# Sign of the first two w_in blocks: a second integer instruction on VectorE, or a sign tile by ScalarE and a product by GpSimd

## The chip, the cores and the metric

The kernel runs on one core of one Trainium2 chip. The time is device microseconds from the first to the last instruction, with what lies around them, and one number is the median of several runs. The profile's names are used for the engines: PE (TensorE), DVE (VectorE), ACT (ScalarE), POOL (GpSimd) and SP (SyncE, which here only issues DMAs).

## The reference

Three layers follow each other:

```python
a = softmax(phi, axis=seq)                      # (4, 8, 576, 32)
k_m, v_m = a^T @ k, a^T @ v                     # 32 memory rows of each head
attn = softmax(q @ k_m^T / 8) @ v_m             # (4, 8, 576, 64)
x = attn.transpose(0, 2, 1, 3).reshape(2304, 512)
h = x @ w_in;  g = h * sigmoid(h);  x = g @ w_out          # 512 -> 2048 -> 512
# then a top-2 mixture of 8 experts, 512 -> 1024 -> 512, on x
```

The weights `w_in` (512 x 2048) and `w_out` (2048 x 512) arrive as 64-bit floating point numbers. The kernel reads them as pairs of 32-bit words and makes 32-bit floating point numbers of them on the chip. That conversion is what the change touches.

## The kernel before, in words

The sequence is worked through batch by batch (`b` = 0 to 3). For a batch, the memory rows are formed (`phi_top`, `phi_max`, `memory`, `memory_t`; `KVT[b]` holds them transposed), the attention weights are computed in two column ranges of 256 and 320 tokens (`scores`, `softmax_a`, `softmax_b`, `turn`, `halves`), and w_in is multiplied by the memory's values once per batch (`project`), so that the first MLP product (`mlp_h`, 32 steps of a batch) takes attention weights straight into the 2048 hidden columns. `mlp_x` multiplies the activated hidden rows by w_out. PE keeps precision by splitting its operands into a high and a low part (`ah`, `wph`/`wpl`, `gh`/`gl`, `woh`/`wol`), each product being three matmuls.

w_in is cut into `NP` = 8 blocks of 256 columns, `WI[i]`, and each block into two pieces of 128 x 512 numbers. w_out is cut into 16 pieces of 128 x 512. `stage` (L204) loads a piece as 512 word pairs per partition into one of four `st` buffers. A piece is then narrowed: `shrink` (L209) runs two ScalarE instructions, one on the low words (`lw`), one on the high words (which go into the result `m` as a scaled magnitude); `join` (L215) is a VectorE integer instruction that shifts `m` left by 3 and ors the low bits in. The sign is still missing. It comes in one of two ways, chosen by `own` in `narrow` (L223):

- `own=True` (all of w_in): `sign` (L219), a second VectorE integer instruction, takes the sign bit out of the staged high words and ors it into `m`.
- `own=False` (all of w_out): ScalarE writes the sign of the staged number in bf16 into the tile `cg` (one buffer, L227), and GpSimd multiplies `m` by `cg` (L232).

Block 0 of w_in is not narrowed through `narrow_win` but written out by hand at L858 to L870, between the pieces of the first batch's attention, since the first `project(0, 1)` needs it. `narrow_win(1)` follows at L885, the remaining blocks are narrowed from a table of steps while the MLP of batch 0 runs. After narrowing, a block is written to `win_d` by a DMA that GpSimd issues (L868, L250), for the later batches.

The order on each engine is made from the program's order by a scheduler when the kernel is built; `tc.issue_after` places an instruction behind another one. Each engine works through its own list in order.

Of the kernel before, what the change touches and what calls it, by code (L numbers as in the profile page):

```python
# [6 lines left out]
F32 = mybir.dt.float32  # L7
F32R = mybir.dt.float32r
BF16 = mybir.dt.bfloat16
I32 = mybir.dt.int32  # L10
U32 = mybir.dt.uint32
AF = mybir.ActivationFunctionType
# [32 lines left out]
def body(ctx, tc, a):  # L45
    nc = tc.nc
    pe, act, dve, pool, sp = nc.tensor, nc.scalar, nc.vector, nc.gpsimd, nc.sync
# [8 lines left out]
    def psum(tag, bufs):  # L56
        return ps.tile([128, 512], F32, name=tag, tag=tag, bufs=bufs)
# [19 lines left out]
    ap_ = att.enter_context(tc.tile_pool(name="att", bufs=1, side="right"))  # L77

    AT = {}
    QT, KV, KX, PH, KVT, AH, AU = {}, {}, {}, {}, {}, {}, {}  # L80
# [65 lines left out]
    def memory_t(b):  # L146
        pt = psum("aux", 2)
        for t in range(2):
            pe.transpose(pt[:, t * 128:(t + 1) * 128], src[:, t].rearrange("p g d -> p (g d)"), ident)
        KVT[b] = m1.tile([128, 2, 128], F32, name="kvt", bufs=2)  # L150
        act.activation(KVT[b].rearrange("p t j -> p (t j)"), pt[:, :256], AF.Copy)

    def heads(p, b, t, moving):
        for h in range(4):
# [4 lines left out]
    def scores(b, i):  # L159
        t0, w = T0[i], TW[i]  # L160
        p = [psum("aux", 2)[:, :w] for g in range(2)]
        heads(p, b, 0, lambda h: QT[b, h][:, t0:t0 + w])
        if i == 0:
            AT[b] = ap_.tile([128, 2, S // M, M], F32, name="sct", tag="big", bufs=1)
        for g in range(2):
            dve.transpose(AT[b][:, g].rearrange("p a m -> p (a m)")[:, t0:t0 + w], p[g])

    def softmax_a(b, t0, w):
        n = w // M
        t = AT[b][:, :, t0 // M:t0 // M + n, :]  # L170
        mx = ap_.tile([128, 2, S // M], F32, name="smx")[:, :, :n]
        dve.tensor_reduce(mx, t, axis=AX.X, op=OP.max)
        last = dve.tensor_sub(t, t, mx[:, :, :, None].to_broadcast([128, 2, n, M]))
        act.activation(t, t, AF.Exp, scale=0.125)
        return last
# [33 lines left out]
    def shrink(t, m):  # L209
        low = ap_.tile([128, 512], I32, name="lw", bufs=1)  # L210
        act.activation(low, t[:, :, 0].bitcast(U32), AF.Copy, scale=LOW, bias=LOWB)  # L211
        act.activation(m, t[:, :, 1].bitcast(F32), AF.Copy, scale=2.0 ** -112)
        return low

    def join(m, low):  # L215
        mi = m.bitcast(I32)
        return dve.scalar_tensor_tensor(mi, mi, 3, low, op0=OP.logical_shift_left, op1=OP.bitwise_or)  # L217

    def sign(t, m):  # L219
        mi = m.bitcast(I32)  # L220
        dve.scalar_tensor_tensor(mi, t[:, :, 1], -2 ** 31, mi, op0=OP.bitwise_and, op1=OP.bitwise_or)

    def narrow(t, m, own=False):  # L223
        low = shrink(t, m)
        if not own:
            g = ap_.tile([128, 512], BF16, name="cg", bufs=1)
            act.activation(g, t[:, :, 1].bitcast(F32), AF.Sign)  # L227
        join(m, low)
        if own:
            sign(t, m)  # L230
        else:
            pool.tensor_mul(m, m, g)  # L232


    WP, WI, ST = {}, {}, {}
# [10 lines left out]
    def narrow_win(i):  # L246
        WI[i] = m1.tile([128, 4, PW], F32, name="wi", tag="wi", bufs=2)
        for g, t in enumerate(ST.pop(("i", i))):
            narrow(t, WI[i][:, 2 * g:2 * g + 2, :].rearrange("p r f -> p (r f)"), True)
        pool.dma_start(win_d[i], WI[i].rearrange("p r f -> p (r f)"))  # L250

    def project(i, n):
# [19 lines left out]
    def narrow_wout(i):  # L272
        w = ap_.tile([128, DM], F32, name="wo", bufs=2)
        narrow(ST.pop(("o", i)), w)
        act.activation(woh[i], w, AF.Copy)
        (pool if i % 2 else dve).tensor_sub(wol[i], w, woh[i].bitcast(F32))
# [581 lines left out]
    first = ST.pop(("i", 0))  # L858
    WI[0] = m1.tile([128, 4, PW], F32, name="wi", tag="wi", bufs=2)
    parts = [WI[0][:, 2 * g:2 * g + 2, :].rearrange("p r f -> p (r f)") for g in range(2)]  # L860
    narrow(first[0], parts[0], True)
    memory_t(0)
    scores(0, 0)
    low = shrink(first[1], parts[1])
    with tc.issue_after(softmax_a(0, T0[0], TW[0]).ins):
        joined = join(parts[1], low)
    sign(first[1], parts[1])
    pool.dma_start(win_d[0], WI[0].rearrange("p r f -> p (r f)"))  # L868
    with tc.issue_after(joined.ins):
        softmax_b(0, T0[0], TW[0])  # L870
# [13 lines left out]
    with tc.issue_after(ready.ins):  # L884
        narrow_win(1)  # L885
# [6 lines left out]
    for i in range(1, NP):  # L892
        if i + 1 < NP:
            at(max(0, 4 * i - 7), fetch_win, i + 1)
            at(max(0, 4 * i - 4), narrow_win, i + 1)
        at(4 * i - 2, project, i, 1)
# [5 lines left out]
    for b in range(1, B):  # L902
# [6 lines left out]
        if b == 1:  # L909
            for step, fn, g in ((7, phi_top, 0), (9, phi_max, 0), (9, phi_top, 1), (11, phi_max, 1),  # L910
                                (12, memory, 0), (13, memory, 1)):
                at(step, fn, b, g)
            for step, fn, *more in ((16, memory_t), (20, scores, 0), (23, scores, 1), (24, softmax_a, 0, S),
                                    (25, softmax_b, 0, S), (27, split, 0, 0, S), (28, split, 1, 0, S)):
                at(step, fn, b, *more)
        else:
            at(s + 8, phi_top, b, 0)
            at(s + 9, phi_top, b, 1)
            at(s + 10, phi_max, b, 0)
            at(s + 10, phi_max, b, 1)  # L920
            at(s + 11, memory, b, 0)
            at(s + 11, memory, b, 1)
            at(s + 12, memory_t, b)
            at(s + 15, scores, b, 0)
            at(s + 16, scores, b, 1)
            at(s + 17, softmax_a, b, 0, S)
            at(s + 20, softmax_b, b, 0, S)
            at(s + 22, split, b, 0, 0, S)
            at(s + 24, split, b, 1, 0, S)
# [4 lines left out]
    for b in range(B - 1):  # L934
# [7 lines left out]
        if b == 1:  # L942
            j = TILES.index((b, 4))
# [37 lines left out]
    while s < total + LAG + 6:  # L981
# [4 lines left out]
        if s in (2 * SB, 4 * SB):  # L986
            b = s // SB - 1
# [83 lines left out]
```

## Time and profile before

| | |
|---|---|
| median of 3 runs | 845.61 us (845.02 to 845.68) |
| the profiled execution, its own time | 845.91 us |
| its span, first to last instruction | 844.1 us, 14185 instructions |
| PE busy | 807.1 us, 96% |
| DVE busy | 496.8 us, 59% |
| ACT busy | 360.8 us, 43% |
| POOL busy | 209.9 us, 25% |
| PE's granted clock, mean | 0.983 |

The shares of the table are over the whole span. The profile also has the span in 40 slices, each about 21 us long. PE is busy for 4, 5 and 8 tenths of the first three and for nearly all of every one behind them; its clock is at half in the second. DVE and ACT are busiest in slices 2 to 7, in which the 32 pieces of w_in and w_out are narrowed. The change lies in the first 42 us.

### The profile page before, as it was taken

To read this page: it belongs to the slowest core of one execution; us is meant where nothing else is said; L and a number is where in the kernel's file an instruction comes from. 1 tells how busy PE (TensorE), PEld (TensorE's weight loads), DVE (VectorE), ACT (ScalarE), POOL (GpSimd) and SP (SyncE) were. 2 spreads that over 40 slices of the span, in tenths; PEclk is the share of its full clock that TensorE was granted. 3 is DMA by queue.
4 is the path that set the end of the run, shared out by engine and by line. 5 is a ranking of instruction groups with operands and counts; after the bars stand their busy time and mean duration, and the time that the engine had idled before them with its cause. 6 is when DMAs were issued, how large, how long until landed. Compare 5 with 4: busy or idle time off the path is not lost.

```text
span 844.1 us, 14185 instructions
## 1 busy us (share of the span) xinstructions
PE 807.1 (96%) x5260; PEld 691.4 (82%) x5260; DVE 496.8 (59%) x1178; ACT 360.8 (43%) x856; POOL 209.9 (25%) x237
## 2 busy tenths in 40 slices
PE   4589999999999999999999999999999999999996
PEld 2267678878887888887988989989989899898995
DVE  4898996884268747655724555354553654546521
ACT  3689975444333454553414433324332333233410
POOL 1254530021000400400541504215133142241301
PEclk9599999999999999999999999999999999999999
DMA  9889852543074215232456893765748647586201
GB/s 304 291 295 325 283 217 71 159 131 94 7 229 153 51 51 151 57 82 50 113 138 187 257 257 124 185 237 171 188 169 221 241 139 160 198 220 196 74 4 53
DMA packets 85935, 137.84 MB, mean 163 GB/s; under 512 B 14045, under 2 KB 48349, under 8 KB 85856
## 3 DMA queue, kind: packets, MB, share of 16 engines
q1 hardware_dynamic: 74656, 104.41, 40.9%
q0 software_dynamic: 11200, 32.43, 12.7%
q8 instruction: 43, 0.70, 0.4%
q14 instruction: 36, 0.29, 0.1%
HBM read 106.13 MB, written 31.26 MB: 163 GB/s over the span
## 4 chain that ended last, share of the span: by engine, by line
PE 81%; DVE 9%; ACT 4%; DMA 3%; issue 2%; POOL 1%; SPq 0%; POOLq 0%; ACTq 0%; DVEq 0%
PE x L706 25%; PE x L313 18%; PE x L682 13%; PE h L682 12%; PE h L288 9%; PE aux L157 2%; DMA st<-moe_w_out 1%; DVE th L293 1%; DVE gl L298 1%; DMA kx<-kx 1%; ACT lw L211 1%; POOL wo L232 1%; DMA st<-moe_w_in 1%; DVE mx L113 1%; DVE wo L217 1%
## 5 line engine op out<-in xcount | busy, mean ns | idle before, releaser
L706 PE MATMUL x<-w,gh 128*128 128x512 f32 (+1 forms) x608 | 188.1, 390 | 0.0
L706 PEld LDWEIGHTS x<-w,gh 128*128 128x128 f32 (+1 forms) x608 | 112.4, 186 | 24.3
L682 PE MATMUL h<-xh,w 128*128 128x304 f32 (+4 forms) x512 | 118.7, 304 | 0.0
L706 PE MATMUL x<-w,gl 128*128 128x512 f32 (+1 forms) x304 | 118.5, 390 | 0.0
L682 PE MATMUL x<-xh,w 128*128 128x304 f32 (+4 forms) x512 | 118.1, 302 | 0.0
L288 PE MATMUL h<-ah,wph 128*128 128x320 f32 (+1 forms) x512 | 109.3, 302 | 3.8 <-DVE th L293 1.7
L313 PE MATMUL x<-gh,woh 128*128 128x512 f32 x256 | 105.5, 412 | 0.0
L288 PEld LDWEIGHTS h<-ah,wph 128*128 128x128 f32 x512 | 90.0, 192 | 18.2 <-ACT ah L195 3.6
L721 POOL DMA_INDIRECT out<-y,tab x40 | 41.9, 1049 | 243.1 <-DVE y L716 187.3
L313 PE MATMUL x<-gl,woh 128*128 128x512 f32 x256 | 100.7, 393 | 0.7 <-DVE gl L298 0.7
L313 PE MATMUL x<-gh,wol 128*128 128x512 f32 x256 | 101.2, 395 | 0.0
L293 DVE SCALAR_TENSOR_TENSOR th<-th,h 128x256 f32<-128x256 f32 (+1 forms) x128 | 57.6, 450 | 53.0 <-ACT th L291 52.5
L497 POOL DMA_INDIRECT tab_d<-rows,slot x36 | 40.6, 1128 | 191.3 <-DVE slot L494 177.9
L682 PEld LDWEIGHTS h<-xh,w 128*128 128x128 f32 x512 | 87.3, 188 | 0.6
L682 PEld LDWEIGHTS x<-xh,w 128*128 128x128 f32 x512 | 87.4, 188 | 0.0
L291 ACT ACTIVATE th<-h 128x256 f32<-128x256 f32 (+1 forms) x128 | 52.3, 408 | 73.4 <-PE h L288 71.3
L288 PE MATMUL h<-ah,wpl 128*128 128x256 f32 (+1 forms) x256 | 76.6, 300 | 2.3 <-DVE wpl L264 2.3
L682 PE MATMUL x<-xl,w 128*128 128x304 f32 (+4 forms) x256 | 78.0, 305 | 0.0
L682 PE MATMUL h<-xl,w 128*128 128x304 f32 (+4 forms) x256 | 77.7, 303 | 0.0
L297 ACT ACTIVATE gh<-th 128x256 fp32r<-128x256 f32 x128 | 53.3, 416 | 55.7 <-DVE th L293 55.3
L298 DVE TENSOR_TENSOR gl<-th,gh 128x256 fp32r<-128x256 f32 x120 | 55.1, 459 | 32.0 <-ACT gh L297 28.1
L716 DVE SCALAR_TENSOR_TENSOR y<-x,tab,ex 128x512 f32<-128x512 f32 (+2 forms) x35 | 26.2, 749 | 71.4 <-PE x L706 71.4
(189 smaller groups left out, 1342.0 us busy)
## 6 DMA issues: line engine op xcount, KB each, us to landing
w2s<-moe_w SPq DMA_DIRECT2D x32, 512.0 KB, 8.5
wi<-win_d SPq DMA_DIRECT2D x24, 512.0 KB, 5.1
w1s<-moe_w SPq DMA_DIRECT2D x24, 512.0 KB, 6.2
kv<-kv SPq DMA_DIRECT2D x16, 520.0 KB, 7.3
st<-moe_w_in SPq DMA_DIRECT2D x16, 512.0 KB, 5.2
st<-moe_w_out SPq DMA_DIRECT2D x16, 512.0 KB, 5.9
xs_d<-ex SPq DMA_DIRECT2D x25, 256.0 KB, 3.6
x_d<-xs SPq DMA_DIRECT2D x36, 128.0 KB, 2.4
```

The lines of the kernel that those rows point to most:

```text
L157: pe.matmul(p[g][h * M:(h + 1) * M], KVT[b][r, t, h * M:(h + 1) * M], moving(h)[r], start=True, stop=True)
L288: pe.matmul(p[:, :w], wt[:, g, c:c + 128], AH[b, g][at][:, t0:t0 + w], start=(n == 0), stop=(n == 5))
L291: act.activation(th[:, :w], p[:, :w], AF.Tanh, scale=0.5)
L293: dve.scalar_tensor_tensor(u[:, :w], th[:, :w], 1.0, p[:, :w], op0=OP.add, op1=OP.mult)
L297: act.activation(gh, u[:, :256], AF.Copy)
L298: last = (pool if b == 0 and (2 * f + i) % 4 == 0 else dve).tensor_sub(gl, u[:, :256], gh.bitcast(F32))
L313: pe.matmul(X2[key], held, moved, start=(f == 0 and n == 0), stop=(f == NF - 1 and n == 2))
L497: st = pool.indirect_dma_start(out=tab_d, out_offset=bass.IndirectOffsetOnAxis(ap=slot[:, j, k:k + 1], axis=0), in_=rows.bitcast(I32)[:, j ...
L682: pe.matmul(p[:, :w], wt[:, d, c], x[:, d, r], start=(n == 0), stop=(n == 11))
L706: mm = pe.matmul(p, g, w[:, f, :], start=(n == 0), stop=(n == (15 if both else 23)))
L716: done = dve.scalar_tensor_tensor(y, p[:P], w, EX[k, j], op0=OP.mult, op1=OP.add)
L721: st = pool.indirect_dma_start(out=a["out"], out_offset=bass.IndirectOffsetOnAxis(ap=TAB[k][:P, j, 0:1], axis=0), in_=y, in_offset=None, b ...
```

## The change

Blocks 0 and 1 of w_in (four pieces) get their sign in the way of w_out: ScalarE's sign in bf16 into the one `cg` buffer and GpSimd's product. The blocks 2 to 7 stay with VectorE's integer instruction. In the hand-written part, the sign of the first piece is placed behind `memory_t`'s copy on ScalarE. Lines above L223 keep their numbers; those behind are 4 higher (8 behind the hand-written part).

```diff
+    def signs(t):
+        g = ap_.tile([128, 512], BF16, name="cg", bufs=1)
+        act.activation(g, t[:, :, 1].bitcast(F32), AF.Sign)
+        return g
+
     def narrow(t, m, own=False):
         low = shrink(t, m)
-        if not own:
-            g = ap_.tile([128, 512], BF16, name="cg", bufs=1)
-            act.activation(g, t[:, :, 1].bitcast(F32), AF.Sign)
-        join(m, low)
         if own:
+            join(m, low)
             sign(t, m)
         else:
+            g = signs(t)
+            join(m, low)
             pool.tensor_mul(m, m, g)
...
-            narrow(t, WI[i][:, 2 * g:2 * g + 2, :].rearrange("p r f -> p (r f)"), True)
+            narrow(t, WI[i][:, 2 * g:2 * g + 2, :].rearrange("p r f -> p (r f)"), i > 1)
...
-    narrow(first[0], parts[0], True)
-    memory_t(0)
+    low = shrink(first[0], parts[0])
+    with tc.issue_after(memory_t(0).ins):
+        g = signs(first[0])
+    join(parts[0], low)
+    pool.tensor_mul(parts[0], parts[0], g)
     scores(0, 0)
     low = shrink(first[1], parts[1])
+    g = signs(first[1])
     with tc.issue_after(softmax_a(0, T0[0], TW[0]).ins):
         joined = join(parts[1], low)
-    sign(first[1], parts[1])
+    pool.tensor_mul(parts[1], parts[1], g)
```

`memory_t` now returns its last instruction, for the `issue_after`.

Three places show how the lists move. The first is DVE from the first join to the first range's division (`wi` is the block of w_in, `sct` the attention scores, `wpl` the projected weights' low part). Before:

```order
L217 SCALAR_TENSOR_TENSOR wi<-wi,lw 128x512
L221 SCALAR_TENSOR_TENSOR wi<-st,wi 128x512
L166 STREAM_TRANSPOSE sct<-aux 128x256 x2
L172 TENSOR_REDUCE smx<-sct 128x2x8
L173 TENSOR_TENSOR sct<-sct,smx 128x2x256
L217 SCALAR_TENSOR_TENSOR wi<-wi,lw 128x512
L221 SCALAR_TENSOR_TENSOR wi<-st,wi 128x512
L181 TENSOR_REDUCE ssm<-sct 128x2x8
L264 TENSOR_TENSOR wpl<-aux,wph 128x256
L182 TENSOR_SCALAR ssm<-ssm 128x2x8
L264 TENSOR_TENSOR wpl<-aux,wph 128x256
L183 RECIPROCAL ssm<-ssm 128x2x8
```

And now:

```order
L217 SCALAR_TENSOR_TENSOR wi<-wi,lw 128x512
L166 STREAM_TRANSPOSE sct<-aux 128x256 x2
L172 TENSOR_REDUCE smx<-sct 128x2x8
L173 TENSOR_TENSOR sct<-sct,smx 128x2x256
L217 SCALAR_TENSOR_TENSOR wi<-wi,lw 128x512
L181 TENSOR_REDUCE ssm<-sct 128x2x8
L182 TENSOR_SCALAR ssm<-ssm 128x2x8
L183 RECIPROCAL ssm<-ssm 128x2x8
L268 TENSOR_TENSOR wpl<-aux,wph 128x256
L184 TENSOR_TENSOR sct<-sct,ssm 128x2x256
L268 TENSOR_TENSOR wpl<-aux,wph 128x256
```

Both signs are gone, and the softmax's division (L184) now stands between the two `wpl` instead of behind them.

The second is POOL from its first work on data on (`wo` is a piece of w_out). Before:

```order
L868 DMA win_d<-wi 128x1024
L232 TENSOR_TENSOR wo<-wo,cg 128x512
L184 TENSOR_TENSOR sct<-sct,ssm 128x2x320
L250 DMA win_d<-wi 128x1024
L298 TENSOR_TENSOR gl<-th,gh 128x256
```

And now:

```order
L869 TENSOR_TENSOR wi<-wi,cg 128x512
L875 TENSOR_TENSOR wi<-wi,cg 128x512
L876 DMA win_d<-wi 128x1024
L236 TENSOR_TENSOR wo<-wo,cg 128x512
L236 TENSOR_TENSOR wi<-wi,cg 128x512 x2
L184 TENSOR_TENSOR sct<-sct,ssm 128x2x320
L254 DMA win_d<-wi 128x1024
L302 TENSOR_TENSOR gl<-th,gh 128x256
```

Two products stand ahead of the first write to `win_d`, and two more ahead of the second range's softmax division (L184).

The third is ACT from w_out's first piece to the first tanh (`woh` is that piece's high part). Before:

```order
L227 ACTIVATE cg<-st 128x512
L212 ACTIVATE wi<-st 128x512
L211 ACTIVATE lw<-st 128x512
L275 ACTIVATE woh_89<-wo 128x512
L212 ACTIVATE wi<-st 128x512
L174 ACTIVATE sct<-sct 128x2x320
L291 ACTIVATE th<-h 128x256
```

And now:

```order
L225 ACTIVATE cg<-st 128x512
L212 ACTIVATE wi<-st 128x512
L211 ACTIVATE lw<-st 128x512
L279 ACTIVATE woh_89<-wo 128x512
L225 ACTIVATE cg<-st 128x512
L174 ACTIVATE sct<-sct 128x2x320
L212 ACTIVATE wi<-st 128x512
L211 ACTIVATE lw<-st 128x512
L225 ACTIVATE cg<-st 128x512
L295 ACTIVATE th<-h 128x256
```

The sign of block 1's first piece takes the place of its second piece's first instruction ahead of the exponential, and that piece's three instructions now stand between the exponential and the first tanh.

## Rows read from the trace of the kernel before

**Rows 1.** Busy time by stage: us, busy us (instructions) per engine, clock, DMA.

```profile
17.00:23.00 6.00, 2.59 (x28) 0.67 (x32) 4.96 (x9) 2.83 (x6) 0.00 (x0) 0.54 0.91 325
27.20:37.60 10.40, 4.16 (x23) 1.84 (x23) 9.35 (x19) 8.46 (x17) 3.68 (x4) 0.50 0.95 296
...
45.00:55.00 10.00, 8.81 (x59) 6.73 (x59) 10.00 (x18) 8.62 (x21) 3.72 (x4) 1.00 0.90 282
55.00:65.00 10.00, 9.31 (x54) 7.08 (x53) 9.76 (x20) 8.76 (x22) 5.41 (x5) 1.00 0.85 309
65.00:75.00 10.00, 9.54 (x123) 7.24 (x122) 9.43 (x23) 9.35 (x24) 4.85 (x5) 1.00 0.93 318
75.00:90.00 15.00, 14.87 (x101) 11.51 (x102) 11.94 (x27) 13.49 (x33) 6.72 (x8) 1.00 0.98 333
```

**Rows 2.** Chain that ended last, 15 to 50 us: start, us, what.

```profile
21.46 0.70 DVE wi L217
22.18 0.70 DVE wi L221
...
22.93 1.15 PE aux L157 x8
24.08 0.37 ACT wph L263
...
35.05 1.45 POOL sct L184
36.52 0.52 DVE att L188
...
37.59 3.05 PE h L288 x11
```

**Rows 3.** Groups by line and form, 15 to 130 us: busy, mean ns | idle.

```profile
L221 DVE SCALAR_TENSOR_TENSOR wi<-st,wi 128x512 int32<-128x512 int32 x16 | 11.5, 716 | 0.1
...
L227 ACT ACTIVATE cg<-st 128x512 bf16<-128x512 f32 x16 | 10.8, 675 | 0.0
...
L232 POOL TENSOR_TENSOR wo<-wo,cg 128x512 f32<-128x512 f32 x16 | 19.5, 1221 | 13.5 <-DVE wo L217 9.7 <-ACT th L291 1.5 <-ACT cg L227 1.3
```

**Rows 4.** Timeline, 17 to 30 us: start, duration, engine, line, tiles.

```profile
17.80 0.69 DVE L217 SCALAR_TENSOR_TENSOR wi<-wi,lw 128x512 int32<-128x512 int32 x1 [2.40 <-ACT wi L212]
...
18.10 1.11 PE L157 MATMUL aux<-q,kvt 64*32 64x256 f32 x16 [1.74 <-ACT kvt L151]
...
19.32 0.78 DVE L166 STREAM_TRANSPOSE sct<-aux 128x256 f32<-128x256 f32 x2
...
24.95 1.72 PE L157 MATMUL aux<-q,kvt 64*32 64x320 f32 x16 [0.94 <-DVE wpl L264]
...
28.64 0.69 DVE L217 SCALAR_TENSOR_TENSOR wo<-wo,lw 128x512 int32<-128x512 int32 x1 [0.18 <-ACT wo L212]
...
29.49 1.15 POOL L232 TENSOR_TENSOR wo<-wo,cg 128x512 f32<-128x512 f32 x1 [5.55 <-DVE wo L217]
```

**Rows 5.** Timeline, 31 to 38 us.

```profile
31.77 0.72 ACT L174 ACTIVATE sct<-sct 128x640 f32<-128x640 f32 x1
...
33.95 0.69 DVE L217 SCALAR_TENSOR_TENSOR wi<-wi,lw 128x512 int32<-128x512 int32 x1
```

**Rows 6.** Timeline of POOL and DVE, 43 to 50 us.

```profile
43.12 1.19 POOL L232 TENSOR_TENSOR wo<-wo,cg 128x512 f32<-128x512 f32 x1
43.20 1.19 DVE L307 TENSOR_TENSOR gc<-th,gc 128x64 fp32r<-128x64 f32 x1
...
46.04 1.64 DVE L217 SCALAR_TENSOR_TENSOR wo<-wo,lw 128x512 int32<-128x512 int32 x1
...
49.20 0.21 DVE L307 TENSOR_TENSOR gc<-th,gc 128x64 fp32r<-128x64 f32 x1
```

**Rows 7.** Busy time by stage around PE's change of clock; columns as in rows 1.

```profile
37.50:41.40 3.90, 3.25 (x12) 2.90 (x12) 3.15 (x6) 2.90 (x8) 0.31 (x1) 0.50 0.98 366
41.40:45.00 3.60, 2.91 (x13) 2.08 (x14) 3.57 (x8) 3.18 (x9) 1.77 (x2) 1.00 0.87 287
```

More of the change, by code (lines that the diff above doesn't have):

```diff
@@ L150, in memory_t @@
         KVT[b] = m1.tile([128, 2, 128], F32, name="kvt", bufs=2)
-        act.activation(KVT[b].rearrange("p t j -> p (t j)"), pt[:, :256], AF.Copy)
+        return act.activation(KVT[b].rearrange("p t j -> p (t j)"), pt[:, :256], AF.Copy)
     def heads(p, b, t, moving):
```

## The prediction

> **What bounds the kernel now.** I read the busy time by stage first. From 75 us on PE is the bound: it is busy for 14.87 of 15 us between 75 and 90, at the full clock [rows 1]. What PE has lost by then is lost for good, unless it waits less later. Before that it is not PE: between 45 and 75 DVE is busy for 29.2 of 30 us and ACT for 26.7 [rows 1], as every piece of the two weight matrices passes through both. And before 38 us PE waits for single steps: it is busy for 4.16 of 10.4 us between 27.2 and 37.6, while DVE shows 9.35 [rows 1]. In that head the length of a chain counts. The chain that ended last shows which [rows 2]: the second piece of block 0 is joined (21.46) and signed (22.18) on DVE, at 22.93 PE starts the second half of the projection, at 24.08 ACT takes its high part. Later POOL divides the second range's softmax (35.05), DVE turns it (36.52), and at 37.59 PE begins the dense stretch of MLP matmuls. So the change has to be followed to two points: how late PE starts at 22.93, and how late at 37.59.
>
> **What is removed and added.** Four signs of 0.716 us leave DVE, 2.86 us in all. Four ScalarE signs of 0.675 us (2.70 us) and four POOL products of 1.22 us (4.88 us) are added [rows 3]. A sign on its own chain thus becomes a product that is longer by 0.5 us, plus a handover: from the end of a join at 29.33 to the product at 29.49 is 0.16 us [rows 4]. I take 1.15 us for a product in this head, as the first one shows [rows 4], and 1.22 as the upper end.
>
> The Trainium skill (GPSIMD Engine Reference, section Engine selection) speaks against such a move: it keeps elementwise work on VectorE, since GpSimd is about 2 times slower with two inputs. The trace has 1221 against 716 ns, a ratio of 1.7 [rows 3]; by the page's ratio each product would take an estimated 1.43 us, some 0.2 us more for each one that lies on the chain.
>
> **First piece of block 0.** The join still ends at 18.49 (17.80 + 0.69). Its sign is covered: the transposes behind it on DVE start at 19.32 because PE's scores run from 18.10 to 19.21 [rows 4]. Taking it away gives nothing. The new sign on ACT stands behind `memory_t`'s copy, at whose end the scores start (18.10), and ends one sign later, near 18.7, the product runs from about 18.85 to 20.0. The first half of the projection can start at 20.0 in place of the end of the first transpose at 19.7, which is hidden: its second half waits longer.
>
> **Second piece of block 0.** Its sign on ACT may write `cg` only after the first product (20.0), so it ends at about 20.7, and waits for nothing else; the join, placed behind the softmax, stays at 21.46 to 22.15 [rows 2]. The product runs from 22.31 to 23.46, and PE starts at 23.5 in place of 22.93: **0.6 us late**. DVE gains the sign's place, and the sum of the first range moves up by 0.5 us, but `wpl` behind it still waits for PE and ACT. By the new list the division (0.70 us) stands between the two `wpl`, so the second of these ends near 26.45 in place of 25.3, and the next scores, which need both buffers, end near 27.35 where they ended at 24.95 + 1.72 = 26.67 [rows 4]: 0.7 late. Most of this is covered by ACT, which works on w_out's first piece: the join of that piece at 28.64 waited for ACT [rows 4], and ACT is late by only some 0.15. So the second range's softmax starts about 0.15 us late.
>
> **Block 1.** ACT's order is changed so that a sign (0.68) takes the place of a conversion (0.65) ahead of the exponential: that goes from 31.77 to about 31.95 [rows 5]. The first join, which stands ahead of the exponential's sum and moves by as much, ends at about 32.75, its product runs from 32.9 to 34.05. The second join cannot start before ACT has made both of its inputs, about 33.85 (33.95 before [rows 5]), and a two-input DVE operation that meets a POOL product waits for its end (below), so it runs from 34.05 to 34.75. Two signs were taken from DVE here, but only the wait for ACT takes their place. The second sign on ACT needs `cg` back at 34.05 and ends at 34.8; the second product runs from 34.95 to 36.1. POOL works in order, and the division of the second range stands behind it: it starts at 36.1 where it did at 35.05 [rows 2]. **1.05 us late**, and with it the turn, and PE's dense stretch: 38.65 in place of 37.59.
>
> **From 38 to 75 us.** Here the delay meets an engine with no room. DVE had 0.75 us to spare between 37.5 and 41.4 (3.15 of 3.90 [rows 7]); that takes up part of the 1.05. ACT's first tanh, now behind three instructions of block 1, is not in the chain. The lists of DVE and ACT are reordered in some places up to about 120 us. The DVE work from 42 us on is the same, so I expect DVE to be later by what its spare time did not take, 0.3 to 0.5 us, and PE to follow it: **+0.5 us**. The bounds: nothing, if all of it is taken up by waits of PE before 75 us (0.46 us between 65 and 75 alone [rows 1]); and 1.2 us, the whole of the delay with the longer products, if none is. I take 0.5, since the rows around 45 to 75 show DVE full.
>
> The staged buffers come free earlier (18.7 and 20.7 in place of 19.2 and 22.9, where their signs ended), so two loads start 0.5 and 2.2 us earlier. I cost this at nothing: engines hardly wait for loads here. If that cover went, it would be a gain of less than 1 us.
>
> **The sum.** The profiled execution took 845.91 us, 0.30 more than the median of 845.61. 845.91 + 0.5 = 846.4 in its terms, 846.1 against the median. 0.2% of this kernel is 1.7 us, about what a measurement can tell from no change.
>
> **Rival 1, slower: PE's clock comes back later.** PE ran at half its clock (1.2 of 2.4 GHz) up to 41.4 us and at full behind [rows 7]; it had been dense since 37.59, in front of which it waited. With its dense stretch starting a microsecond later, the rise may come later too. What it would cost: between 41.4 and 45 PE did 2.91 us of matmuls at full clock with 0.7 us of waiting [rows 7]; at half they would take up to 5.8, so up to 2.2 us more than there was room for, and some of it was bound by DVE and not PE: about 1.5. With the 0.5 to 1.2 that makes +2.0 to +2.7, 847.6 to 848.3. It decides when PE's work between 38 and 41.4 is too little for the rise; my walk leaves 2.75 us of it (41.4 - 38.65) against the 3.25 of before, which speaks against it, as one more product or a longer wait in front speaks for it. Chance 0.2.
>
> **Rival 2, faster: DVE's stalls fall away.** Several DVE operations with two inputs in SBUF took far longer next to a POOL operation. The subtraction at 43.20 took 1.19 us beside the product from 43.12, and 0.21 us at 49.20; the join at 46.04 took 1.64 in place of 0.69 [rows 6]. These two cost 0.98 and 0.95 us of the fullest engine. The new order of DVE's list may miss them, and then the gain would be up to 1.9 less the 0.5 above, and more if the 1.05 is absorbed too: 843.7 to 844.2. Against it: the same products stand on POOL, and a shift makes new meetings as well as it undoes old ones. The Trainium skill (SBUF — State Buffer, section Who interferes with whom) says that a VectorE instruction with two SBUF inputs and a GpSimd instruction that reads SBUF exclude each other, and the second to issue waits; the rows of 43 us agree. Chance of a gain over 1.7 us 0.13.
>
> **Rival 3, nothing: the delay is absorbed.** All of it goes into PE's later waits, and the time stays at 845.6. In favour: PE waits in the head and DVE is relieved of 2.86 us. Against: the relief falls where DVE waits for ACT and POOL. Chance 0.22, inside "the same". That the change does not do what it says is excluded: the lists show four signs fewer on DVE and four products more on POOL.
>
> **How the numbers follow.** A small delay (my forecast, 0.3 to 1.5 us) has 0.41, absorbed 0.22: 0.63 for within 0.2%. Rival 1 with 0.2 and other mishaps of the reordered lists with 0.04 make 0.24 for slower; rival 2 has 0.13. The range reaches from 844.3, the mild end of rival 2, to 847.9, inside rival 1.
>
> **What would show it.** Right: the second half of the first projection starts near 23.5; the POOL division near 36.1 behind two products; PE's first 320-column matmul near 38.65; the clock rising at about the same place; the DVE stretch at 45 to 55 us still full. Wrong: the division at 35 or earlier (then the products do not stand in the way), a rise of the clock well behind 42 us (rival 1), or DVE rows near 43 and 46 us without their long durations and PE ahead of before at 75 us (rival 2).

## The result, and the profile after

The changed kernel takes 850.39 us (median of 9 runs, 848.69 to 852.04), the kernel before on the same chip 845.32 us (9 runs, 844.80 to 846.64). The ratio is 1.0057, with a 95% interval of 1.0047 to 1.0067. So the change costs 5.1 us. In two of the later sets of runs before itself took 850.4 and 850.8 us, in the others 844.7 to 845.3 (the 5 us between them arise near 340 and 450 us, in every kernel), so each ratio below is taken against before in the same set and on the same chip. The forecast was 846.1 us and its range ended at 847.9: **it was wrong**, and by much more than the delays that it had walked through.

The profiled execution took 850.53 us. Its page begins so; the last line is of the DMA queues (packets, MB, share of 16 engines):

```profile
span 848.7 us, 14188 instructions
PE 806.7 (95%) x5260; PEld 692.9 (82%) x5260; DVE 493.9 (58%) x1174; ACT 364.5 (43%) x860; POOL 212.5 (25%) x241
...
q14 instruction: 37, 0.30, 0.1%
```

The page of before has one packet fewer there, which matters below:

```profile
q14 instruction: 36, 0.29, 0.1%
```

DVE is busy for 2.9 us less, as its four signs make, ACT for 3.7 and POOL for 2.6 us more. (The added products are 4.6 us, four of 1.15 or 1.16; the rest of POOL's work came out 2.0 us shorter, and why was not followed.) PE did no more work than before (806.7 against 807.1 us), so the time lies in its waits, or behind its end.

**The head came nearly as forecast.** The timeline of the changed kernel, 17 to 38 us (start, duration, engine, line, operation; in brackets the idle time before it and what ended it):

```profile
18.72 1.16 POOL L869 TENSOR_TENSOR wi<-wi,cg 128x512 f32<-128x512 f32 x1 [15.67 <-ACT cg L225]
...
21.87 1.15 POOL L875 TENSOR_TENSOR wi<-wi,cg 128x512 f32<-128x512 f32 x1 [1.99 <-ACT sct L174]
...
23.07 1.08 PE L157 MATMUL aux<-wi,kvt 64*32 64x256 f32 x8 [2.45 <-POOL wi L875]
...
32.41 1.16 POOL L236 TENSOR_TENSOR wi<-wi,cg 128x512 f32<-128x512 f32 x1 [2.14 <-DVE wi L217]
...
34.36 1.16 POOL L236 TENSOR_TENSOR wi<-wi,cg 128x512 f32<-128x512 f32 x1 [0.79 <-ACT cg L225]
35.47 1.27 POOL L184 TENSOR_TENSOR sct<-sct,ssm 128x640 f32<-128x640 f32 x1
```

The second half of the first projection starts at 23.07 (forecast 23.5; 22.93 in [rows 2]) and waits for the product. The division starts at 35.47 behind two products (forecast 36.1; 35.05 in [rows 2]). PE's dense stretch starts at 37.84 (forecast 38.65; 37.59 in [rows 2]). The head has cost 0.25 us. At 60.7 us, ahead of the first loss below, the lag between the two rows of the tanh's product shown there is still 0.26 us; whether it stays to the end is what kernel a_pin shows further down.

**The first loss: two waits of PE near 62 and 104 us.** Busy time by stage of the changed kernel (columns as in [rows 1]):

```profile
61.00:64.00 3.00, 1.13 (x8) 0.93 (x8) 3.00 (x6) 2.93 (x7) 1.16 (x1) 1.00 1.03 381
65.00:68.00 3.00, 3.00 (x8) 2.42 (x9) 2.81 (x8) 1.90 (x7) 1.74 (x2) 0.50 0.78 210
...
104.00:109.00 5.00, 2.54 (x26) 1.47 (x25) 4.06 (x9) 3.74 (x10) 2.40 (x2) 1.00 0.95 325
```

And the same stretches before:

```profile
61.00:64.00 3.00, 2.87 (x21) 2.16 (x22) 2.92 (x6) 3.00 (x8) 0.95 (x1) 1.00 1.01 399
65.00:68.00 3.00, 2.89 (x21) 1.93 (x20) 3.00 (x8) 3.00 (x10) 1.77 (x2) 1.00 0.78 220
...
104.00:109.00 5.00, 5.00 (x37) 3.77 (x38) 4.08 (x9) 4.63 (x11) 3.03 (x3) 1.00 1.00 400
```

PE is busy for 1.13 of 3 us where it was busy for 2.87, and behind that its clock is at half (0.50, 1.2 of 2.4 GHz): 8 matmuls in 3 us against 21, of which 8 are short ones (L157). Near 104 us it is busy for 2.54 of 5 us against 5.00. Behind this second wait its clock fell again in the profiled execution, and did not in after_again, another execution of the same kernel:

```profile
109.00:113.00 4.00, 4.00 (x15) 3.42 (x14) 4.00 (x9) 3.68 (x10) 2.48 (x2) 0.57 0.90 298
```

```profile
109.00:113.00 4.00, 4.00 (x27) 3.35 (x21) 3.60 (x7) 3.68 (x10) 1.87 (x2) 1.00 0.90 313
```

The timeline shows what it waited for at the first place, in the changed kernel:

```profile
60.72 0.41 DVE L297 SCALAR_TENSOR_TENSOR th<-th,h 128x256 f32<-128x256 f32 x1
...
61.06 0.68 DVE L217 SCALAR_TENSOR_TENSOR wi<-wi,lw 128x512 int32<-128x512 int32 x1
...
61.66 0.68 DVE L280 TENSOR_TENSOR wol<-wo,woh 128x512 fp32r<-128x512 f32 x1
...
61.77 1.16 POOL L302 TENSOR_TENSOR gl<-th,gh 128x256 fp32r<-128x256 f32 x1 [1.05 <-ACT gh L301]
62.26 1.22 DVE L221 SCALAR_TENSOR_TENSOR wi<-st,wi 128x512 int32<-128x512 int32 x1
...
63.40 0.28 DVE L120 TENSOR_REDUCE mt<-aux 128x1 f32<-128x128 f32 x1
...
63.73 0.49 PE L122 MATMUL aux<-ident,mt 128*128 128x128 f32 x2 [1.69 <-DVE mt L120]
```

And before:

```profile
60.46 0.41 DVE L293 SCALAR_TENSOR_TENSOR th<-th,h 128x256 f32<-128x256 f32 x1
...
60.79 0.28 DVE L120 TENSOR_REDUCE mt<-aux 128x1 f32<-128x128 f32 x1
...
61.13 0.49 PE L122 MATMUL aux<-ident,mt 128*128 128x128 f32 x2 [0.67 <-DVE mt L120]
```

The reduction of `mt` (0.28 us of work, in `phi_max` of batch 1) stood directly behind the tanh's product. Now three other instructions stand between: a join, `wol`, and a sign of a later block, which takes 1.22 us in place of 0.7, beside POOL's `gl` (61.77 to 62.93), as the DVE rows beside POOL in [rows 6] did. PE works in order, and waits 1.69 us.

At the second place PE's scores of batch 1 wait for `wpl`, the low part of a projection. Changed kernel:

```profile
104.15 0.65 ACT L225 ACTIVATE cg<-st 128x512 bf16<-128x512 f32 x1
...
105.62 0.41 DVE L297 SCALAR_TENSOR_TENSOR th<-th,h 128x256 f32<-128x256 f32 x1
106.06 0.42 ACT L301 ACTIVATE gh<-th 128x256 fp32r<-128x256 f32 x1 [1.26 <-DVE th L297]
106.39 0.64 ACT L267 ACTIVATE wph<-aux 128x256 fp32r<-128x256 f32 x2
...
106.93 0.74 DVE L268 TENSOR_TENSOR wpl<-aux,wph 128x256 fp32r<-128x256 f32 x2
107.40 1.10 PE L157 MATMUL aux<-q,kvt 64*32 64x320 f32 x16 [2.46 <-DVE wpl L268]
```

Before:

```profile
103.12 0.64 ACT L263 ACTIVATE wph<-aux 128x256 fp32r<-128x256 f32 x2
...
103.52 0.76 DVE L264 TENSOR_TENSOR wpl<-aux,wph 128x256 fp32r<-128x256 f32 x2
103.64 0.42 ACT L297 ACTIVATE gh<-th 128x256 fp32r<-128x256 f32 x1
...
104.00 1.10 PE L157 MATMUL aux<-q,kvt 64*32 64x320 f32 x16 [0.67 <-DVE wpl L264]
```

The two `wph` stood ahead of `gh` on ACT. Now they stand behind a sign and behind `gh`, which waits 1.26 us for DVE. The wait of PE is 2.46 us in place of 0.67.

Part of what PE loses at the two places is made up, because it waits less elsewhere: between 58 and 130 us its other waits for `wpl`, in `mlp_h`, are shorter (total, times, longest, us), before

```profile
PE h L288 <- DVE wpl L264: 2.3, 2, 1.2
```

and now

```profile
PE h L292 <- DVE wpl L268: 0.8, 1, 0.8
```

The rest stays lost, since PE is the bound behind. I measure it as the time from batch 0's first scores on PE (18.10 before, [rows 4]; 18.11 now) to the 34th tanh of ACT: before

```profile
131.62 0.44 ACT L291 ACTIVATE th<-h 128x320 f32<-128x320 f32 x1 [0.69 <-PE h L288]
```

and now

```profile
134.18 0.44 ACT L295 ACTIVATE th<-h 128x320 f32<-128x320 f32 x1 [0.85 <-PE h L292]
```

So the middle is late by (134.18 − 18.11) − (131.62 − 18.10) = 2.55 us, and it is still so at the 128th tanh, at 385 us.

**The second loss: behind the last write.** The last data instruction of the program is a write to `out` that POOL issues. In before it starts 5.5 us ahead of the span's end (844.1), in the changed kernel 8.0 us (848.7):

```profile
838.63 0.97 POOL L721 DMA_INDIRECT out<-y,tab  x1 [4.47 <-DVE y L716]
```

```profile
840.75 0.97 POOL L725 DMA_INDIRECT out<-y,tab  x1 [4.47 <-DVE y L720]
```

In between POOL has only semaphore instructions. The first two of them behind that write start 0.06 us apart in before and 2.33 us apart in the changed kernel. So +2.5 us come after all the work is done. The sum of the two profiled spans: 2.55 (from batch 0's first scores to the 128th tanh, the head among it) − 0.43 (from there to the last write; five of the six later profiles from sets in which before took about 845 us, those of a_block0 and a_pin_cap among them, show the same against this one execution of before, whatever their lists, and why is open) + 2.47 (end) = 4.6, which is 848.7 − 844.1.

### The profile page after: what moved, and what is told of

Read it like the earlier page. It is cut to its first block, busy times and chain, and to the rows that moved or that the text cites. A ratio compares the mean times of both kernels' runs of the same rounds, so it can differ in the third digit from the quotient of the medians.

```text
span 848.7 us, 14188 instructions
## 1 busy us (share of the span) xinstructions
PE 806.7 (95%) x5260; PEld 692.9 (82%) x5260; DVE 493.9 (58%) x1174; ACT 364.5 (43%) x860; POOL 212.5 (25%) x241
## 4 chain that ended last, share of the span: by engine, by line
PE 85%; DVE 8%; DMA 2%; ACT 2%; issue 1%; POOL 0%; SPq 0%; POOLq 0%; ACTq 0%
PE x L710 25%; PE x L317 20%; PE x L686 12%; PE h L686 12%; PE h L292 10%; PE aux L157 2%; DVE gl L302 1%; DMA st<-moe_w_out 1%; DMA kx<-kx 1%; DMA st<-moe_w_in 1%; DVE mx L113 1%; DVE th L297 1%; PE aux L136 1%; DVE wo L217 1%; DVE wi L217 1%
```

## The experiments

Two theories follow from these rows for the middle: **the lists** (PE's waits come from the order that the scheduler made, not from the added signs and products) against **the work** (the added instructions delay the middle themselves); and for the end, **the length of POOL's program** against the products as such. In the built program POOL has 707 instructions before and 715 now: four products, each with a wait.

All runs together. "Middle" is scores to 34th tanh less that of before, "end" the time from the start of the last write to the end of the span. With the lists of before the middle scatters by some 0.4 us between executions (b_pool4, b_pool8), with those of the changed kernel by 1 us, and there PE's clock differs: where it falls to half once between 60 and 131 us, the middle is 1.8 to 2.1 (after_again, a_pool8, b_pin); where it falls twice it is 2.5 (changed), and in a_capmerge, where it stays at half about twice as long (63 to 70 us), 2.7.

| kernel | lists from 41 us | POOL instr. | PE waits, mt / wpl, us | middle, us | end, us | ratio to before |
|---|---|---|---|---|---|---|
| before | before | 707 | 0.7 / 0.7 | 0 | 5.5 | 1 |
| changed | changed | 715 | 1.7 / 2.5 | +2.5 | 8.0 | 1.0057 [1.0047, 1.0067] |
| after_again | changed | 715 | 1.7 / 2.5 | +1.9 | 7.6 | 1.0059 [1.0045, 1.0073] |
| b_pool4 | before | 711 | 0.6 / 0.6 | −0.1 | 5.6 | 1.0003 [0.9993, 1.0012] |
| a_pool8 | changed | 723 | 1.7 / 2.5 | +2.1 | 7.7 | 1.0069 [1.0052, 1.0086] |
| a_mt_first | a third order | 716 | 1.1 / 2.0 | +8.4 | 7.5 | 1.0143 [1.0126, 1.0160] |
| a_both | a third order | 724 | 1.0 / 1.9 | +11.1 | 7.3 | 1.0122 [1.0105, 1.0139] |
| a_pin | before | 715 | 0.7 / 0.6 | −0.3 | 7.7 | 1.0038 [1.0024, 1.0052] |
| b_pin | changed | 707 | 1.7 / 2.5 | +1.8 | 5.7 | 1.0034 [1.0023, 1.0045] |
| a_capmerge | changed | 711 | 1.7 / 2.5 | +2.7 | 5.3 | 1.0040 [1.0028, 1.0051] |
| b_pool8 | before | 715 | 0.7 / 0.6 | −0.4 | 7.5 | 1.0030 [1.0016, 1.0044] |
| a_mt_only | changed, 1 row moved | 715 | none / 2.5 | +1.0 | 7.7 | 1.0046 [1.0033, 1.0059] |
| a_two | changed, 5 rows moved | 715 | none / 1.5 | 0.0 | 7.9 | 1.0036 [1.0023, 1.0050] |
| a_block0 | nearly before | 711 | 0.6 / 0.7 | −1.2 | 5.4 | 0.9995 [0.9986, 1.0004] |
| a_block1 | nearly changed | 711 | 2.1 / 2.7 | +2.2 | 5.5 | 1.0031 [1.0019, 1.0043] |
| a_pin_cap | before | 711 | 0.7 / 0.7 | +0.1 | 5.4 | 1.0006 [0.9997, 1.0014] |

**First attempts: longer programs, and mt ahead.** Kernel b_pool4 is before with four small fills more on POOL (its edit is shown), a_pool8 the changed kernel with eight more:

```diff
+    idle = const.tile([128, 4], F32, name="idle")
+    for i in range(4):
+        pool.memset(idle[:, i:i + 1], float(i))
```

> Four one-column memsets are added at the start of GpSimd's list, where it idles for over 10 us; no other engine's list changes, so the work and its order are those of before. Theory A (GpSimd's instruction stream is longer by four instructions, and a load of instructions, in queue q14 of the profile, falls into the last semaphore steps and stalls them): slower by about 2.0 us, all of it behind the last write of the output; the lag against before is 0 up to 838 us. Rival (the last 2 us of the changed kernel are a consequence of its late PE, or chance): no difference, within 0.3 us.

> The changed kernel with eight one-column memsets at the start of GpSimd's list; no other engine's list changes. Theory A: the instruction stream's boundary moves by eight more instructions, out of the last semaphore steps, and the 2.0 us behind the last write of the output go: 848.4 in place of 850.4 us. Rival (chance or a consequence of the late PE): still 850.4, the gap of 2.3 us between two semaphore steps still there.

Both missed: four fills more bring no stall, and eight more on top of the changed kernel do not take it away. That left a threshold between 711 and 715 instructions, tested below. Kernel a_mt_first puts the reduction ahead with a constraint to the scheduler, a_both has it and the eight fills:

```diff
+    def behind(b, g, fn, *args):
+        with tc.issue_after(MT[b, g].ins):
+            fn(*args)
+
+    hooks[8].remove((narrow_win, (4,)))
+    hooks[9].remove((phi_max, (1, 0)))
+    hooks[9][0:0] = [(phi_max, (1, 0)), (behind, (1, 0, narrow_win, 4))]
```

> The changed kernel with the reduction for the second batch's maximum (L120) put directly behind the tanh product on VectorE, where it stood before, with block 4's narrowing behind it. Theory B (PE's wait of 1.69 us for that reduction near 62 us, and the fall of its clock behind it, make the middle's 2.5 us): no such wait, no fall of the clock at 65 us, the 12th tanh at 66.4 us or earlier in place of 68.9, and the time 2 to 2.5 us less than the changed kernel's, some 848.2 us, as the tail's 2 us stay. Rival (ScalarE's four more instructions or the products on GpSimd cost it): the 12th tanh is still more than 1.5 us later than before.

> The last two together: eight memsets and the reduction put first. If both theories hold and the effects add: 850.4 - 2.0 - 2.5 = 845.9 us, the time of before within 0.7 us. If one of them fails: 848 or more.

Both missed too. PE's wait for `mt` fell to 1.1 us, but the time got worse by far (1.0143): the scheduler answered the constraint with a third order, in which PE waits in more places and the middle is 8.4 us late. The experiment moved more than the row that it meant to move. What it says on the theory is little; what it says on method is that one row can be tested only with all others held.

**The lists crossed.** So the order was held: a table of instruction names for each of PE, DVE, ACT and SP (215, 150, 171 and 35 instructions, about 41 to 130 us), each chained behind the one ahead of it on its engine, for the order alone. Kernel a_pin is the changed kernel with the order of before from 41 us on, b_pin is before with the order of the changed kernel. POOL's list was not held; in the traces it comes out the same but for the four products:

```diff
+    pins = {
...
+    }
+    named = {i.name: i for i in nc.cur_bb.bb.instructions}
+    for row in pins.values():
+        for x, y in zip(row, row[1:]):
+            tc.add_manual_dep(named[f"I-{y}"], f"I-{x}", mybir.DependencyInfo(
+                mybir.DependencyClass.NoSync, mybir.DependencyReason.DATA), reason="issue_after")
```

> The changed kernel up to 41 us, and from there the order of the instructions on PE, DVE, ACT and SP as the kernel before has it, written out as a table; the work is the same as in the changed kernel. Theory A (the middle's 2.5 us are the reordered lists, the other 2.1 us are a stall at the end): PE does not wait for the reduction of mt at 62 us by more than some 0.7 us, its clock does not fall at 65, work around 130 us is within 0.6 us of before; the end's gap of 2.1 to 2.3 us stays; ratio to before 1.002 to 1.003. Theory B (the added signs and products themselves delay the middle): 130 us is 2 us or more behind before, ratio 1.005 to 1.006.

> The kernel before up to 41 us, with VectorE's signs, and from there the order of the lists of the changed kernel. Theory A (reordered lists): PE waits some 1.7 us for the reduction of mt near 62 us, its clock falls behind that, 130 us comes 2 to 3 us behind before, no gap at the end; ratio 1.0025 to 1.0035. Theory B (added work): no such wait, ratio 1.000 with bounds of 0.001.

PE's waits of a_pin between 58 and 130 us (total, times, longest, us):

```profile
...
PE aux L122 <- DVE mt L120: 0.7, 1, 0.7
PE aux L157 <- DVE wpl L268: 0.6, 1, 0.6
```

and of b_pin:

```profile
PE aux L157 <- DVE wpl L264: 2.5, 1, 2.5
PE aux L122 <- DVE mt L120: 1.7, 1, 1.7
```

The waits go with the lists and not with the work. With before's order the changed head is 0.3 us ahead at the 34th tanh; with the changed order the old head is 1.8 us late (2 to 3 expected, so this one came out small); its end is that of before (5.7 us), so the ratio of 1.0034 is not from there. The theory of the work falls. Both ratios stand for some 1 us more than these profiles show: a_pin's 1.0038 (3.2 us; expected 1.002 to 1.003) against 2.2 us of end, b_pin's 1.0034 (2.9 us) against 1.8 us of middle. Both differences lie inside the intervals, and no run explains them.

**The end.** Kernel b_pool8 is before with eight fills in place of four (715 instructions, as the changed kernel). Kernel a_capmerge is the changed kernel with eight fills of its own merged into four:

```diff
-        for i, w in enumerate(COLS + (CAP,)):
-            pool.memset(cap[:, i:i + 1], float(w))
+        for i, j, w in ((0, 2, COLS[0]), (2, 5, COLS[2]), (5, 7, COLS[5]), (7, 8, CAP)):
+            pool.memset(cap[:, i:j], float(w))
```

> The kernel before with eight one-column fills of GpSimd more at the start, all other lists unchanged; GpSimd's program is as long as the changed kernel's. Theory A' (length): a gap of 2.1 to 2.3 us behind the last write, nothing else, ratio 1.0025. Rival (the gap belongs to the products or to the other lists): ratio 1.000, as with four fills more.

> The changed kernel with eight one-column fills of GpSimd merged into four, all other lists unchanged; GpSimd's program is 4 instructions shorter than the changed kernel's, 4 longer than that of before. Theory A' (the gap at the end depends on the length of GpSimd's program, and comes between 4 and 8 instructions more than before): the gap of 2.1 to 2.3 us behind the last write goes, the middle stays 2.5 us late, ratio 1.003. Rival (the gap belongs to the products, whatever the length): it stays, ratio 1.0055.

From the page of b_pool8, and behind it from its timeline:

```profile
span 851.8 us, 14193 instructions
...
q14 instruction: 37, 0.30, 0.1%
```

```profile
844.25 0.97 POOL L724 DMA_INDIRECT out<-y,tab  x1 [4.47 <-DVE y L719]
```

And of a_capmerge:

```profile
span 852.8 us, 14184 instructions
...
q14 instruction: 36, 0.29, 0.1%
```

```profile
847.50 0.97 POOL L725 DMA_INDIRECT out<-y,tab  x1 [4.47 <-DVE y L720]
```

Eight fills and nothing else bring the stall to before (851.8 − 844.25 = 7.5 us), and four instructions fewer take it from the changed kernel (852.8 − 847.50 = 5.3). Both came as expected; the expected ratios, 1.0025 and 1.003, lie inside the intervals of the measured ones. Over all sixteen profiles the end is 5.3 to 5.7 us with 711 POOL instructions or fewer, and 7.3 to 8.0 with 715 or more, whatever else differs. **The length of POOL's program decides, not the products.** That holds between 707 and 724 instructions; whether the stall goes away again in a longer program was not tried.

**One row, then two places.** With every list of the changed kernel held, a_mt_only moves the reduction of `mt` three rows up on DVE. Kernel a_two moves, besides, two `wph` on ACT (ahead of the sign and `gh`) and two `wpl` on DVE (ahead of `gl`), as before has them.

> The changed kernel with one instruction of one list elsewhere: VectorE's reduction of mt (L120, batch 1) stands directly behind the tanh's product in place of three rows later; every other row of every list is held as the changed kernel has it. Theory A1 (this one row makes the middle's delay): PE's wait for it near 62 us falls from 1.7 to some 0.7 us, no clock fall behind it, work at 130 us is within 1 us of before; with the end's 2.2 us the ratio is 1.002 to 1.0035. Rival A2 (other rows behind it delay as much, it is the sum of many): the wait goes, but 130 us is still 1.5 to 3 us behind before, ratio 1.0045 to 1.006.

> The changed kernel with two places of its lists as before: VectorE's reduction of mt directly behind the tanh's product, and, near 104 us, the two high parts of the projection (wph) directly behind woh on ScalarE and the two low parts (wpl) directly behind the tanh's product on VectorE, in place of behind one more sign, the hidden rows' high part and their subtraction. Every other row is held as the changed kernel has it. With the first place alone 130 us was 1.16 us behind before, and PE waited 2.5 us for wpl near 104 us. Theory A3 (two places make the middle): PE's wait there falls to 0.7 to 1.7 us, 130 us is between 0.5 us ahead of before and 0.6 us behind it, and with the end's 2.2 us the ratio is 1.002 to 1.0035. Rival (the rows behind are as late whatever stands there): 130 us stays 1 us or more behind, ratio 1.004 to 1.005.

> The changed kernel itself on the chip of this call, so that what the two places give back is read against it on one chip: ratio 1.0045 to 1.007, PE's waits of 1.7 us for mt and 2.5 us for wpl, 130 us between 2 and 3.3 us behind before, the gap of 2.1 to 2.5 us at the end.

One row of 0.28 us gives back 0.9 to 1.6 us of the middle (+1.0 against +1.9 and +2.5), and PE does not wait for it any more; its clock stays at full near 65 us and falls behind the second wait, as in the changed kernel. The first theory, that this row is all, fell short: the wait for `wpl` stayed at 2.5 us, and the ratio is 1.0046 where 1.0035 was the most that it allowed. With the second place the middle is back at 0.0, and PE's clock does not fall again between 47 and 840 us. PE's wait there is still 1.5 us, 0.8 more than in before, so a wait does not add to the middle one for one. Against after_again on the same chip a_two is faster by 850.02 − 847.95 = 2.1 us. Of the rest of its ratio, 1.0036 or 3.0 us, the end is 2.4 (7.9 against 5.5); the other 0.6 lies inside the interval. So the middle hangs on five rows; how it divides between PE's waits and the falls of the clock behind them was not separated.

**Each half of the change, and both causes taken away.** Kernel a_block0 changes block 0 alone, a_block1 block 1 alone, and a_pin_cap is a_pin with the four merged fills.

The edit of a_block0 against the changed kernel:

```diff
-            narrow(t, WI[i][:, 2 * g:2 * g + 2, :].rearrange("p r f -> p (r f)"), i > 1)
+            narrow(t, WI[i][:, 2 * g:2 * g + 2, :].rearrange("p r f -> p (r f)"), True)
```

and that of a_block1, where the hand-written part of block 0 stands as before (the first piece; the second likewise):

```diff
-    low = shrink(first[0], parts[0])
-    with tc.issue_after(memory_t(0).ins):
-        g = signs(first[0])
-    join(parts[0], low)
-    pool.tensor_mul(parts[0], parts[0], g)
+    narrow(first[0], parts[0], True)
+    memory_t(0)
```

> Only block 0 of w_in gets the new sign; block 1 keeps VectorE's second integer instruction. PE's list is that of before, GpSimd's program is 4 instructions longer than before's. Theory A: no reordering of weight on VectorE, no gap at the end: ratio 1.000, between 0.999 and 1.001. Rival (added work in the head costs): 130 us is 0.5 us or more late, ratio 1.001 or more.

> Only block 1 of w_in gets the new sign, block 0 keeps VectorE's. GpSimd's program is 4 instructions longer than before's; the lists behind 41 us are reordered as in the changed kernel but for some 20 rows (mt's reduction stands behind one row in place of three). Theory A: no gap at the end; the middle late by 0.5 to 2.5 us, ratio 1.0005 to 1.003. Rival (block 1's signs cost nothing and all comes from block 0): 130 us on time, ratio 1.000.

> The changed kernel with both causes taken away: the lists of before from 41 us on, and four fills of GpSimd fewer. Theory A: no gap at the end, 130 us between 0.6 us ahead of before and 0.3 us behind it: ratio 1.000, between 0.999 and 1.0015. If a third cause is left, 1.002 or more. No theory has it faster than before by over 0.2%.

Block 0 alone leaves PE's list as it was, and costs nothing (0.9995 [0.9986, 1.0004]): its profile is even 1.2 us ahead in the middle, but the time cannot be told from before's. Block 1 alone brings both long waits (2.1 and 2.7 us), no stall at the end, and 1.0031. The reordering thus hangs on block 1. With before's order and the shorter program the changed kernel takes 845.23 against 844.91 us, 1.0006 [0.9997, 1.0014]: no third cause is left that could be measured, holding the lists in order costs nothing that shows, and no version beats before by what a measurement can tell.

## Why the prediction was wrong

- **"The second half of the first projection 0.6 us late", "the division 1.05 us late", "PE's dense stretch 38.65": right in kind, somewhat large.** Measured +0.14, +0.42 and +0.25 us. In this execution the first scores ran at the full clock (0.67 us in place of 1.11 [rows 4]), which helped. In after_again they took 1.11 us as before, and counted from their start (18.50) the three came 0.55, 0.81 and 0.64 us later than in before.
- **"DVE's spare time takes up part of it, PE follows by 0.5 us": the absorption was right and the term of 0.5 us too large.** a_pin has the whole of the changed head and is 0.3 us ahead of before at the 34th tanh, a_pin_cap is 0.1 us behind. The head costs nothing that could be measured.
- **"The DVE work from 42 us on is the same, so I expect DVE to be later by what its spare time did not take": this step failed.** The work is the same, its order is not. I had said that the lists are reordered up to about 120 us, and had priced that at nothing, with a chance of 0.04 for all its mishaps. b_pin shows that the order alone costs 1.8 us in the middle, a_two that five rows make it (PE's wait for `mt` grew from 0.67 to 1.69 us, that for `wpl` from 0.67 to 2.46). The lists of before and of the change had these rows in them; I read them at three places of the head, and not where PE waits for a short instruction of DVE.
- **The end was not in the prediction at all.** Four products with four waits were costed as time on POOL's engine, never as length of its program. They cost 2.1 to 2.5 us that way, nearly half of the result.
- **Rival 1 (the clock's rise comes later): it happened in some executions, and its price was wrong.** The clock rose at 40.9 us in the profiled execution of the changed kernel. In six of the ten profiles with the changed head it rose at 45 to 47 us, and in one of the four with the head of before as well (b_pool8, at 45.3), so these profiles do not tell whether the change has a part in it. In a_pin it rose 5 us later than in before: between 41.4 and 45 us, where [rows 7] have it at full, it was at half, and PE was the busiest engine, while behind that PE was busier than the 8.81 us of 45 to 55 us in [rows 1]:

```profile
41.40:45.00 3.60, 3.40 (x10) 3.02 (x11) 2.94 (x6) 3.23 (x10) 1.74 (x2) 0.50 1.01 286
45.00:55.00 10.00, 9.78 (x62) 7.83 (x61) 10.00 (x18) 8.63 (x21) 3.70 (x4) 0.92 0.92 283
```

Nothing of it was left at the 34th tanh (−0.3 us): what PE lost up to 45 us it made up in time that it had spent waiting. The 1.5 us that I gave it is not there. The clock mattered elsewhere: it fell behind the long wait at 62 us, and in some executions behind that at 104.

- **Rival 2 (DVE's stalls fall away): no.** They moved. In the changed kernel the subtraction near 44 us is short (the one ahead of it, `gl` at 43.10, takes 1.28 us beside a product), the join behind it long as before (1.64 in [rows 6]), and the sign at 62.26 stalled in the worst place:

```profile
44.31 0.21 DVE L311 TENSOR_TENSOR gc<-th,gc 128x64 fp32r<-128x64 f32 x1
...
45.45 1.55 DVE L217 SCALAR_TENSOR_TENSOR wo<-wo,lw 128x512 int32<-128x512 int32 x1
```

- **Rival 3 (all absorbed)** would have been right of the head, and was wrong of the kernel.

## What to carry to other kernels

Where a scheduler orders the lists, an edit in one place is an edit of every list behind it: compare the lists up to the last row that differs, and look in them for short instructions on whose result the bounding engine waits, above all where longer work that nobody waits for yet now stands ahead. To learn what such an order costs, hold all lists and move a row; a constraint on one row lets the scheduler move the rest. And look at what lies behind the last write: eight more instructions on one engine lengthened it here by 2 us (four did not), and merging eight small fills into four took that away.

## What the runs showed of the hardware

The stall at the end was not expected. With 711 POOL instructions or fewer, POOL's first two semaphore instructions behind the last write start 0.06 to 0.07 us apart in all seven profiles, with 715 or more 2.1 to 2.5 us apart in all nine. The profile shows packets of instruction code on queue 14, 8 KB each (0.29 MB in 36), and in the nine a further packet comes right behind the stall, at 5.9 us or more after the last write's start, where in the seven the last comes at 4.1 or earlier. It starts 0.7 to 0.9 us after the stall has ended, so it is not itself what ended it; one or two packets start at 3.1 to 4.1 us, about where the stall starts, in all sixteen. In the changed kernel, from 842 us to the end:

```profile
q14 instruction: 4, 0.03, 1.4%
```

That POOL waits there for its own code to be fetched is argued from this and not shown: the profile does not name what ended the wait. The Trainium skill (DMA: Bandwidth & Descriptors, section Queues, rings and completion order) gives row 14 of the queues to the runtime, refills among its uses, and the label "instruction" in the trace agrees, though queue 8 carries it too (43 packets, 0.70 MB, in before).

Behind a wait of PE of 1.7 to 2.1 us for `mt` its clock fell to half near 65 us (0.50 in the window above), in all six runs with a wait of that length (changed, after_again, b_pin, a_capmerge, a_pool8, a_block1); in a_mt_only and a_two, where the wait is gone, it did not. Behind the second wait it is not so plain: with 2.5 to 2.7 us for `wpl` the clock fell again near 107 to 113 us in three of seven runs (changed, a_mt_only, a_block1) and stayed at full in four (after_again, a_pool8, b_pin, a_capmerge). What else decides it the runs do not show.

Why the scheduler puts the reduction behind the three rows when block 1's signs change was not tried.
